# RetNet attention and a maxout FFN: last products in the order the pairs were finished, weights converted two pieces at a time

## The chip, the cores and the metric

One core of a Trainium2 chip runs the whole kernel. The metric is device time in microseconds, the median over several executions. A core has TensorE (PE; its weight loads are shown apart as PEld), VectorE (DVE), ScalarE (ACT), GpSimd (POOL), and SyncE (SP), which here only issues DMAs. Each engine executes its own list of instructions in order, and semaphores tie the lists together.

## The reference

```python
batch, n_heads, seq, head_dim = (8, 8, 576, 64)
scores = scale * np.matmul(q, k.transpose(0, 1, 3, 2))      # scale = 1/sqrt(64)
Dmat = np.where(rel >= 0, gamma[:, None, None] ** rel[None, :, :], 0.0)   # rel = i - j, one gamma per head
ret = scores * Dmat[None, :, :, :]
attn = np.matmul(ret, v)
x = attn.transpose(0, 2, 1, 3).reshape(4608, 512)
h = np.maximum(np.maximum(x @ w1, x @ w2), x @ w3)          # w1, w2, w3: (512, 768)
out = h @ w_out                                            # w_out: (768, 512)
```

q, k and v are float32. The four weight matrices are float64; the kernel gets them as 64-bit integers, the bits of the doubles, and makes float32 of them on the chip.

## The kernel before

The 4608 rows are nine tiles of 512 tokens (`t` = 0 to 8). For each tile, attention makes `xT[t]`, and `ffn(t)` makes the hidden units `h` and the output rows. The 768 hidden units are six blocks of 128, called `fb`, or three pairs of blocks, called `fp`. The order of instructions on every engine is the order in which the Python code emits them (`tc.manual_schedule()`): `ffn(t)` is a generator that emits a stretch of its own work at each step, and `steps(t + 1)` puts the attention of the next tile between the steps. TensorE goes through attention of the next tile and the FFN of this tile in turn.

**Tile 0** does plain products. For every unit (`fp`, `i`), where `i` is one of the three matrices, `up_plain` multiplies two blocks (L744), ScalarE copies the first matrix's result to `h` (L749), and VectorE takes the maximum with the next two (L748). Then `downs_plain` multiplies `h` by `w_out` (L731). Meanwhile the weights are loaded and converted, in the order in which tile 0 uses them: 24 `pieces` of 128 x 512, 18 of `w1` to `w3` and 6 of `w_out`. `load_weights` issues their DMAs from SP (L504, two for a piece; L499 for `w_out`) into six buffers named `bits`. `convert_all` is a generator that emits the conversion step by step; `convert(n)` takes n of its steps, and `ffn(0)` calls it between the blocks. One piece takes:

- VectorE, L629: `expo`, the exponent bits of the high word; ScalarE, L630: `mant` = 1 + low word x 2^-52
- ScalarE, L632 and L635: two Relus that turn `expo` into the exponent of a float32, saturating at both ends; VectorE, L634: `frac`, the top 20 fraction bits
- VectorE, L640: `mant` += `frac` x 2^-20 ("whole"); L645: the sign bit is put into `expo` ("sign"); L651: `w` = `mant` x `expo` ("product"), after which `load_weights(1)` asks for the next piece

Each is 128 x 512. The first two pieces go one by one; from the third on, two pieces get their masks first and are then finished one after the other.

**Tiles 1 to 8** use fewer products. `weight_sums`, `sums_of_x` and the list `PRODUCTS` make the three maxed products of a pair `fp` from sums of weights and of x (L720, evicted at L705, joined on VectorE at L708); the last joins of a pair end its `h`. Tile 1 does pair 1 in the plain way, and its pairs in the order 1, 0, 2; later tiles take 0, 2, 1 (`order` in `ffn`, L785). Then `sums_of_hidden` (L530 to L532) makes four sums `H1` to `H4` of h for each pair, and `downs(t, h)` makes the output with seven products of 256-wide halves (L562), in the order 1, 2, 6, 7, 5, 4, 3. Product n runs over the three pairs, in `product`; products 1, 2 and 4 read `h` itself, the others the sums:

```python
        def product(n, out, first):
            for fp in range(NF // 2):
                for m, cols, o in out:
                    nc.tensor.matmul(o, lhsT=hS[n](fp)[:, m * P:(m + 1) * P], rhs=late["T"][n][:, fp, cols], ...
```

One float32 matmul of the program appears as two passes of TensorE in the trace, so product 1 (bank `dx`) is 3 pairs x 2 blocks x 2 = 12 passes of 256 columns; in the last tile its second block is split, and there are 18.

Of the kernel before, what the change touches and what calls it, by code (L numbers as in the profile page):

```python
# [77 lines left out]
WAHEAD = 6  # L78
# [3 lines left out]
def kernel(  # L82
# [14 lines left out]
    nc = tc.nc  # L97
    P = 128
    B, H, S, D = q.shape
    N, DM = out.shape  # L100
# [4 lines left out]
    NF = DF // P  # L105
# [25 lines left out]
    one, top, inf, first = (const.tile([P, 1], FP32, name=n) for n in ("one", "top", "inf", "first"))  # L131
# [354 lines left out]
    units = [(fp, i) for fp in range(NF // 2) for i in range(3)]  # L486
    pieces = [(i, 2 * fp + e) for fp, i in units for e in range(2)] + [("out", fb) for fb in range(NF)]
    w_sb, bits, to_load = {}, {}, deque(pieces)
    w_up = [const.tile([P, NF, DM], FP32, name=f"w{i}") for i in range(3)]
    w_out = const.tile([P, NF // 2, 2, DM], FP32, name="w_out")  # L490

    def load_weights(n):
        for _ in range(n):
            if not to_load:
                return
            i, fb = piece = to_load.popleft()
            t = bits[piece] = wraw.tile([P, DM], I64, tag="bits", name="bits")
            if i == "out":
                nc.sync.dma_start(t[:], moe_w_out[fb * P:(fb + 1) * P, :])  # L499
            else:  # L500
                heads = WS[i][:, fb * P:(fb + 1) * P].rearrange("(h p) f -> p h f", p=D)
                blocks = t[:].rearrange("p (n f) -> p n f", f=P)
# [28 lines left out]
        urgent.append(lambda: vec(s2, s1, a11, op=ALU.subtract))  # L531
        urgent.append(lambda: (pool(s3, a11, a21, op=ALU.subtract), pool(s4, a12, s2, op=ALU.subtract)))  # L532

    def downs(t, h):

        def raw_hidden(r, e):
            return lambda fp: h[:, 2 * fp + e, NH * r:NH * (r + 1)]
# [19 lines left out]
            return banks.get(id(src), src)  # L557

        def product(n, out, first):
            for fp in range(NF // 2):  # L560
                for m, cols, o in out:
                    nc.tensor.matmul(o, lhsT=hS[n](fp)[:, m * P:(m + 1) * P], rhs=late["T"][n][:, fp, cols],  # L562
                                     start=first and fp == 0 and (m == 0 or last and out is x),
                                     stop=fp == NF // 2 - 1, skip_group_check=True)

        def kept(src):
            both = ppool.tile([P, NM, NH], FP32, tag="part", name="part")
# [51 lines left out]
    def convert_all():  # L619

        def masks(raw_bits):
            words = raw_bits[:].bitcast(I32).rearrange("p (f two) -> p f two", two=2)
            high = words[:, :, 1]
            low = raw_bits[:].bitcast(U32).rearrange("p (f two) -> p f two", two=2)[:, :, 0]
            expo = wtmp.tile([P, DM], I32, tag="expo", name="expo")
            mant = wtmp.tile([P, DM], FP32, tag="mant", name="mant")
            nc.vector.tensor_scalar(out=expo[:], in0=high, scalar1=0x7FF00000, scalar2=None, op0=ALU.bitwise_and)  # L629
            nc.scalar.activation(mant[:], low, AF.Identity, bias=one[:], scale=2.0 ** -52)  # L630
            yield
            nc.scalar.activation(expo[:].bitcast(FP32), expo[:], AF.Relu, bias=top[:], scale=-8.0)  # L632
            frac = wtmp.tile([P, DM], I32, tag="frac", name="frac", bufs=2)
            nc.vector.tensor_scalar(out=frac[:], in0=high, scalar1=0xFFFFF, scalar2=None, op0=ALU.bitwise_and)  # L634
            nc.scalar.activation(expo[:], expo[:].bitcast(FP32), AF.Relu, bias=inf[:], scale=-1.0)  # L635
            yield
            return high, expo, mant, frac

        def whole(mant, frac):
            nc.vector.scalar_tensor_tensor(out=mant[:], in0=frac[:], scalar=2.0 ** -20, in1=mant[:],  # L640
                                           op0=ALU.mult, op1=ALU.add)

        def product(piece, high, expo, mant):
            i, fb = piece
            nc.vector.scalar_tensor_tensor(out=expo[:], in0=high, scalar=-2 ** 31, in1=expo[:],  # L645
                                           op0=ALU.bitwise_and, op1=ALU.bitwise_or)
            if i == "out":
                w = w_sb[piece] = w_out[:, fb // 2, fb % 2, :]
            else:
                w = w_sb[piece] = w_up[i][:, fb, :]  # L650
            nc.vector.tensor_tensor(w, mant[:], expo[:].bitcast(FP32), op=ALU.mult)  # L651
            load_weights(1)

        for group in [pieces[:1], pieces[1:2]] + [pieces[n:n + 2] for n in range(2, len(pieces), 2)]:
            masked = []
            for piece in group:
                masked.append((yield from masks(bits.pop(piece))))
            for piece, (high, expo, mant, frac) in zip(group, masked):
                whole(mant, frac)
# [29 lines left out]
    def convert(n):  # L689
        for _ in range(n):  # L690
            next(converting, None)
# [59 lines left out]
    def ffn(t):  # L751

        h = hpool.tile([P, NF, NT], FP32, tag="h", name="h")
        if t == 0:
            for fp, i in units:
                for fb in (2 * fp, 2 * fp + 1):
                    maximum = up_plain(t, h, fb, i)
                    if CPT not in qks:
                        maximum()
                        transposes(CPT)  # L760
                        convert(4)
                        continue
# [204 lines left out]
```

## Time and profile before

| | |
|---|---|
| median of 4 runs | 757.37 us (756.87 to 758.52) |
| the profiled execution | 758.52 us, span 756.5 us |
| TensorE busy | 747.1 us, 99% of the span, 5928 passes |
| VectorE busy | 535.2 us, 71% |
| ScalarE busy | 342.4 us, 45% |
| GpSimd busy | 90.4 us, 12% |
| granted TensorE clock | 1.0 |
| DMA | 59.2 MB, 78 GB/s on average |

The span runs from the first to the last instruction that the profiler recorded on the core; the execution's own time is longer by 2.0 us. A row of the profile names the line of the kernel, the engine, the operation, the tile written and the tiles read, shapes, and how often; a row of the timeline begins with its start and its length in us, and may end with the engine's idle time before it and, behind the arrow, what ended that. Ends of matmuls are modelled.

### The profile page before, as it was taken

What the parts mean: (1) busy time and instruction counts of PE and PEld (TensorE: products, weight loads), DVE (VectorE), ACT (ScalarE), POOL (GpSimd) and SP (SyncE); (2) the same over time, 40 slices, a digit from 0 to 9 for tenths busy, and PEclk for the clock granted to TensorE, in tenths of its full rate; (3) what the DMA queues carried; (4) which work ended last, traced back from release to release, by engine and by line L of the source; (5) the groups of instructions that cost most, each with busy time, mean ns of one, the idle gap of its engine ahead of it and who ended that gap; (6) DMA issues with size and microseconds to landing.
All of it is one profiled execution on the core that took longest, in us unless ns stands there. A gap on an engine that the chain in (4) does not pass through costs nothing.

```text
span 756.5 us, 15101 instructions
## 1 busy us (share of the span) xinstructions
PE 747.1 (99%) x5928; PEld 608.3 (80%) x5928; DVE 535.2 (71%) x929; ACT 342.4 (45%) x700; POOL 90.4 (12%) x112
## 2 busy tenths in 40 slices
PE   8999999999999999999999999999999999999998
PEld 7645545587888888888888888888888888888887
DVE  2998997958886866686668847685768666863662
ACT  3574651255255534553355345542555255414441
POOL 3110013002010100011011102010101010100000
PEclk9999999999999999999999999999999999999999
DMA  9995752404242514242343224232514141000001
GB/s 218 222 244 127 206 126 75 94 1 80 76 88 45 91 31 105 49 73 55 72 82 66 62 62 93 49 65 66 94 31 92 43 93 35 1 30 28 1 1 55
DMA packets 230310, 59.20 MB, mean 78 GB/s; under 512 B 211168, under 2 KB 228960, under 8 KB 230240
## 3 DMA queue, kind: packets, MB, share of 16 engines
q1 hardware_dynamic: 229664, 57.91, 35.5%
q8 instruction: 46, 0.75, 0.4%
q10 hardware_dynamic: 576, 0.33, 0.2%
q14 instruction: 24, 0.20, 0.1%
HBM read 48.76 MB, written 9.44 MB: 77 GB/s over the span
## 4 chain that ended last, share of the span: by engine, by line
PE 91%; DVE 4%; ACT 1%; DMA 1%; SPq 1%; issue 1%; POOL 0%; DVEq 0%; ACTq 0%; POOLq 0%
PE a L720 16%; PE b L720 14%; PE up L744 11%; PE dx L562 11%; PE c L720 8%; PE dz L562 5%; PE e L720 5%; PE d L720 5%; PE o L438 4%; PE down L731 3%; PE dy L562 3%; PE sk L317 3%; DVE part L708 2%; SPq L218 1%; ACT part L705 1%; PE s L299 1%
## 5 line engine op out<-in xcount | busy, mean ns | idle before, releaser
L708 DVE TENSOR_TENSOR part<-part 128x512 f32<-128x512 f32 x161 | 111.2, 691 | 94.4 <-ACT part L705 92.1
L705 ACT COPY part<-b 128x512 f32<-128x512 f32 x115 | 67.4, 586 | 140.1 <-PE b L720 140.1
L708 DVE TENSOR_TENSOR h<-h,part 128x512 f32<-128x512 f32 x115 | 79.6, 692 | 28.2 <-ACT h L705 24.3
L744 PE MATMUL up<-xT,w 128*128 128x512 f32 (+2 forms) x200 | 84.7, 578 | 1.5 <-DVE w L651 1.5
L705 ACT COPY part<-a 128x512 f32<-128x512 f32 x92 | 53.9, 586 | 48.5 <-PE a L720 48.1
L744 PEld LDWEIGHTS up<-xT,w 128*128 128x128 f32 x200 | 36.8, 190 | 43.5 <-issue 38.7
L720 PE MATMUL a<-s,w 128*128 128x256 f32 x276 | 70.9, 379 | 0.0
L720 PE MATMUL b<-s,n 128*128 128x256 f32 x276 | 70.8, 379 | 0.0
L186 ACT ACTIVATE kraw<-kraw,gk 128x64 f32<-128x64 f32 x208 | 65.6, 346 | 3.6 <-DMA kraw<-in_k_dram 3.3
L720 PEld LDWEIGHTS b<-s,n 128*128 128x128 f32 x276 | 52.4, 190 | 7.1
L720 PEld LDWEIGHTS a<-s,w 128*128 128x128 f32 x276 | 52.4, 190 | 7.1
L532 POOL TENSOR_TENSOR H<-h 128x256 f32<-128x256 f32 x24 | 20.3, 844 | 285.8 <-DVE h L708 285.7
L335 POOL TENSOR_TENSOR va<-va,gs_of 64x512 f32<-64x512 f32 x24 | 25.8, 1075 | 232.2 <-DVE va L333 178.3
L720 PE MATMUL c<-xT,w 128*128 128x256 f32 x184 | 49.1, 389 | 0.0
L720 PE MATMUL d<-s,w 128*128 128x256 f32 x184 | 47.3, 380 | 0.2 <-ACT part L705 0.2
L720 PE MATMUL b<-xT,n 128*128 128x256 f32 x184 | 47.2, 379 | 0.0
L562 PE MATMUL dx<-To,H 128*128 128x256 f32 (+1 forms) x204 | 44.9, 370 | 0.0
L720 PE MATMUL e<-xT,w 128*128 128x256 f32 x184 | 43.5, 379 | 0.0
L720 PE MATMUL a<-xT,n 128*128 128x256 f32 x184 | 43.5, 379 | 0.0
L562 PEld LDWEIGHTS dx<-To,H 128*128 128x128 f32 x204 | 36.6, 190 | 4.9
L720 PEld LDWEIGHTS d<-s,w 128*128 128x128 f32 x184 | 34.9, 190 | 5.3 <-ACT part L705 0.6
L325 DVE TENSOR_TENSOR m<-sk,gm 64x512 f32<-64x512 f32 x56 | 38.5, 687 | 1.0
(122 smaller groups left out, 1338.7 us busy)
## 6 DMA issues: line engine op xcount, KB each, us to landing
bits<-in_moe_w_dram SPq DMA_DIRECT2D x36, 256.0 KB, 5.4
out_dram<-osb SPq DMA_DIRECT2D x35, 256.0 KB, 2.1
kraw<-in_k_dram SPq DMA_DIRECT2D x32, 256.0 KB, 3.0
qraw<-in_q_dram SPq DMA_DIRECT2D x224, 32.0 KB, 2.2
kxraw<-in_k_dram SPq DMA_DIRECT2D x224, 32.0 KB, 2.1
va<-in_v_dram SPq DMA_DIRECT2D x56, 128.0 KB, 3.1
bits<-in_moe_w_out_dram SPq DMA_DIRECT2D x6, 512.0 KB, 5.7
vraw<-in_v_dram SPq DMA_DIRECT2D x7, 256.0 KB, 4.8
```

Source lines behind the costliest of these rows:

```text
L186: scaling.popleft()()
L317: nc.tensor.matmul(sk[c][half(c), h, :], lhsT=kr[half(c), h, :], rhs=vas[g, c][half(c), h, :], start=True, stop=True)
L325: nc.vector.tensor_tensor(ms[g, c][half(c)], sk[1 - c][half(c)], gm[half(c)], op=ALU.mult)
L335: nc.gpsimd.tensor_tensor(to[half(1)], to[half(1)], gs_of[half(1)].unsqueeze(2).to_broadcast([D, H, D]), op=ALU.mult)
L438: nc.tensor.matmul(o[half(c), n % 2, n // 2, half(m)], lhsT=vas[g, m][:, h, :], rhs=ms[g, m][:, h, :], start=m == 0 and n == 0, stop=True, ...
L532: urgent.append(lambda: (pool(s3, a11, a21, op=ALU.subtract), pool(s4, a12, s2, op=ALU.subtract)))
L562: nc.tensor.matmul(o, lhsT=hS[n](fp)[:, m * P:(m + 1) * P], rhs=late["T"][n][:, fp, cols], start=first and fp == 0 and (m == 0 or last and ...
L705: nc.scalar.copy(of[step], ps[step[0]][:])
L708: nc.vector.tensor_tensor(of[dst], a, b, op=op)
L720: nc.tensor.matmul(ps[chain][:, e, :], lhsT=factor(w, 2 * fp + e), rhs=xS[t][x], start=n == 1 and e == 0, stop=ends, skip_group_check=True)
L731: nc.tensor.matmul(b[:], lhsT=h[:, fb, m * P:(m + 1) * P], rhs=w_sb["out", fb], start=(fb == 0), stop=(fb == NF - 1))
L744: nc.tensor.matmul(ps[:, cols], lhsT=w_sb[i, fb][:, dc * P:(dc + 1) * P], rhs=xT[t][:, dc, cols], start=dc == 0 and cols.start == 0, stop= ...
```

## The change

Two edits. In `downs`, `product` takes the pairs in the order given by `ffn`, the one in which the tile finished them, instead of 0, 1, 2; the marks for the first and the last matmul of an accumulation follow. In the conversion, the two pieces of a pair share one tile of `bits`, `expo`, `mant` and `frac`. The first four pieces are still converted with 512-wide instructions, in the same sequence as before. From the fifth piece on, every instruction covers both pieces of a pair, 1024 wide; the exponent mask of the following pair is emitted ahead of the sign and product of the present one; and `convert` is asked for fewer, larger steps. There are half as many buffers of twice the size.

```diff
-    wraw = while_converting.enter_context(tc.tile_pool(name="wraw", bufs=WAHEAD))
-    wtmp = while_converting.enter_context(tc.tile_pool(name="wtmp", bufs=4))
+    wraw = while_converting.enter_context(tc.tile_pool(name="wraw", bufs=WAHEAD // 2))
+    wtmp = while_converting.enter_context(tc.tile_pool(name="wtmp", bufs=2))
...
             i, fb = piece = to_load.popleft()
-            t = bits[piece] = wraw.tile([P, DM], I64, tag="bits", name="bits")
+            if fb % 2 == 0:
+                bits[i, fb // 2] = wraw.tile([P, 2, DM], I64, tag="bits", name="bits")
+            t = bits[i, fb // 2][:, fb % 2, :]
...
-    def downs(t, h):
+    def downs(t, h, order):
...
         def product(n, out, first):
-            for fp in range(NF // 2):
+            for fp in order:
                 for m, cols, o in out:
                     nc.tensor.matmul(o, lhsT=hS[n](fp)[:, m * P:(m + 1) * P], rhs=late["T"][n][:, fp, cols],
-                                     start=first and fp == 0 and (m == 0 or last and out is x),
-                                     stop=fp == NF // 2 - 1, skip_group_check=True)
+                                     start=first and fp == order[0] and (m == 0 or last and out is x),
+                                     stop=fp == order[-1], skip_group_check=True)
...
+        class Two:
+            def __init__(self, n):
+                self.i, fb = pieces[2 * n]
+                self.fp = fb // 2
+                words = bits.pop((self.i, self.fp))[:].rearrange("p e f -> p (e f)")
+                self.high = words.bitcast(I32).rearrange("p (e f two) -> p e f two", e=2, two=2)[:, :, :, 1]
+                self.low = words.bitcast(U32).rearrange("p (e f two) -> p e f two", e=2, two=2)[:, :, :, 0]
+                self.expo = wtmp.tile([P, 2, DM], I32, tag="expo", name="expo")
+                self.mant = wtmp.tile([P, 2, DM], FP32, tag="mant", name="mant")
+
+            def exponent(self, e):
+                expo = self.expo[:, e, :]
+                nc.vector.tensor_scalar(out=expo, in0=self.high[:, e, :], scalar1=0x7FF00000, scalar2=None,
+                                        op0=ALU.bitwise_and)
+                nc.scalar.activation(self.mant[:, e, :], self.low[:, e, :], AF.Identity, bias=one[:], scale=2.0 ** -52)
+
+            def fraction(self, e):
+                expo = self.expo[:, e, :]
+                if e != TWO[1]:
+                    self.frac = wtmp.tile([P, 2, DM], I32, tag="frac", name="frac", bufs=1)
+                nc.scalar.activation(expo.bitcast(FP32), expo, AF.Relu, bias=top[:], scale=-8.0)
+                nc.vector.tensor_scalar(out=self.frac[:, e, :], in0=self.high[:, e, :], scalar1=0xFFFFF, scalar2=None,
+                                        op0=ALU.bitwise_and)
+                nc.scalar.activation(expo, expo.bitcast(FP32), AF.Relu, bias=inf[:], scale=-1.0)
+
+            def whole(self, e):
+                nc.vector.scalar_tensor_tensor(out=self.mant[:, e, :], in0=self.frac[:, e, :], scalar=2.0 ** -20,
+                                               in1=self.mant[:, e, :], op0=ALU.mult, op1=ALU.add)
+
+            def sign(self, e):
+                nc.vector.scalar_tensor_tensor(out=self.expo[:, e, :], in0=self.high[:, e, :], scalar=-2 ** 31,
+                                               in1=self.expo[:, e, :], op0=ALU.bitwise_and, op1=ALU.bitwise_or)
+
+            def product(self, e):
+                if self.i == "out":
+                    w = w_out[:, self.fp]
+                else:
+                    w = w_up[self.i][:, 2 * self.fp:2 * self.fp + 2, :]
+                nc.vector.tensor_tensor(w[:, e, :], self.mant[:, e, :], self.expo[:, e, :].bitcast(FP32), op=ALU.mult)
+                for n in range(2)[e]:
+                    w_sb[self.i, 2 * self.fp + n] = w[:, n, :]
+                    load_weights(1)
...
+        two = Two(2)
+        two.exponent(both)
+        yield
+        two.fraction(both)
+        two.whole(both)
+        yield
+        for n in range(3, len(pieces) // 2 + 1):
+            following = Two(n) if n < len(pieces) // 2 else None
+            if following:
+                following.exponent(both)
+            two.sign(both)
+            yield
+            two.product(both)
+            yield
+            if following:
+                following.fraction(both)
                 yield
-                product(piece, high, expo, mant)
+                following.whole(both)
                 yield
+            two = following
...
-                    convert(4)
+                    convert(4 if (fp, i) == units[0] else 2)
                     maximum()
                 yield
-            convert(6)
+            convert(3)
             for fb, _ in enumerate(downs_plain(t, h)):
-                convert(4 if fb < 2 else 4 * len(pieces))
+                convert(2 if fb < 2 else 4 * len(pieces))
...
-        for n, _ in enumerate(downs(t, h)):
+        for n, _ in enumerate(downs(t, h, order)):
```

The functions that `Two` replaces are `masks`, `whole` and `product` of `convert_all`. In the prediction, "mask" is `exponent` or `fraction` on VectorE, and pair n of the conversion is the one of pieces 2n and 2n + 1, so pair 2 holds the weights of unit (0, 2), pairs 3 to 5 those of units (1, 0) to (1, 2), and pairs 9 to 11 those of `w_out`.

More of the change, by code (lines that the diff above doesn't have):

```diff
@@ L496, in load_weights @@
             i, fb = piece = to_load.popleft()
-            t = bits[piece] = wraw.tile([P, DM], I64, tag="bits", name="bits")
+            if fb % 2 == 0:
+                bits[i, fb // 2] = wraw.tile([P, 2, DM], I64, tag="bits", name="bits")
+            t = bits[i, fb // 2][:, fb % 2, :]
             if i == "out":
-                nc.sync.dma_start(t[:], moe_w_out[fb * P:(fb + 1) * P, :])
+                nc.sync.dma_start(t, moe_w_out[fb * P:(fb + 1) * P, :])
             else:
                 heads = WS[i][:, fb * P:(fb + 1) * P].rearrange("(h p) f -> p h f", p=D)
-                blocks = t[:].rearrange("p (n f) -> p n f", f=P)
+                blocks = t.rearrange("p (n f) -> p n f", f=P)
                 for c in range(2):
@@ L619, in convert_all @@
     def convert_all():
[L623 to L630, printed above, removed]
-            yield
[L632 to L635, printed above, removed]
-            yield
-            return high, expo, mant, frac
@@ L639, in whole @@
[L639 to L659, printed above, removed]
+        class Two:
[35 more added lines that the diff above has]
+                    load_weights(1)
@@ new lines, in convert_all @@
+        TWO = [slice(0, 1), slice(1, 2)]
+        both = slice(0, 2)
+        two = Two(0)
+        for e in TWO:
+            for step in (two.exponent, two.fraction, two.whole):
+                step(e)
+                yield
+            two.sign(e)
+            two.product(e)
+            yield
+        two = Two(1)
+        for e in TWO:
+            for step in (two.exponent, two.fraction):
+                step(e)
+                yield
+        for e in TWO:
+            two.whole(e)
+            yield
+            two.sign(e)
+            two.product(e)
+            yield
@@ L660, in convert_all @@
+        two = Two(2)
[3 more added lines that the diff above has]
+        two.whole(both)
+        yield
+        for n in range(3, len(pieces) // 2 + 1):
[3 more added lines that the diff above has]
+            two.sign(both)
+            yield
+            two.product(both)
+            yield
+            if following:
+                following.fraction(both)
                 yield
-                product(piece, high, expo, mant)
+                following.whole(both)
```

## The prediction

> **What bounds the kernel now.** I read the sums by stretch of time first, then the order of the engines' work in the two places that the change touches, then who waits for whom. (Columns of the first view: stretch, length, then busy time and instructions of TensorE, its weight loads, VectorE, ScalarE and GpSimd, granted clock, DMA share, GB/s.)
>
> ```profile
> 26.00:126.00 100.00, 100.00 (x485) 51.36 (x486) 92.28 (x171) 55.57 (x85) 12.87 (x15) 1.00 0.71 169
> 187.00:734.00 547.00, 546.24 (x4540) 476.91 (x4539) 376.18 (x632) 249.08 (x534) 57.53 (x67) 1.00 0.28 58
> ```
>
> From 26 us on TensorE is never idle by this account, in the first tile (26 to 126, where the weights are converted) and in the tiles from the third on alike; the clock is full. VectorE is at 92% in the first tile and still not the bound. So nothing that shortens VectorE or ScalarE is worth time by itself: the change can only win where TensorE waits inside its "busy" time, and lose where it makes TensorE wait. The ends of matmuls are modelled, so such a wait hides in the length of a row. The timeline of TensorE at the first of the last products (dx, product 1) of tiles 1, 2 and 8 (columns: start, length from first start to last end):
>
> ```profile
> 187.41 2.75 PE L562 MATMUL dx<-w_out,h 128*128 128x256 f32 x12
> ...
> 266.21 3.14 PE L562 MATMUL dx<-w_out,h 128*128 128x256 f32 x12
> ...
> 734.78 3.17 PE L562 MATMUL dx<-w_out,h 128*128 128x256 f32 x18
> ```
>
> The same twelve passes take 2.75 us in tile 1 and 3.14 us in tile 2 (3.15 in each of tiles 3 to 7). The last tile splits its bank, so it is compared with its own later dx rows of 18 passes, 2.80 us. The weight loads and VectorE of tile 2 say why:
>
> ```profile
> 266.00 0.84 PEld L562 LDWEIGHTS dx<-w_out,h 128*128 128x128 f32 x4
> 267.36 1.59 PEld L562 LDWEIGHTS dx<-w_out,h 128*128 128x128 f32 x8 [0.52 <-DVE h L708]
> ```
> ```profile
> 266.62 0.69 DVE L708 TENSOR_TENSOR h<-h,part 128x512 f32<-128x512 f32 x1
> ```
>
> Four passes (pair 0), then a wait for h, the hidden units of the pair finished last, which VectorE ends at 267.31; then the other eight. The waits in total name it once:
>
> ```profile
> PEld dx L562 <- DVE h L708: 3.5, 7, 0.5
> ```
>
> Seven tiles. Tile 1 computes pairs in the order 1, 0, 2 and takes them 0, 1, 2, so its last-finished pair already comes last, and it has no wait. Tiles 2 to 8 compute 0, 2, 1 and take 0, 1, 2.
>
> **Part one: pairs taken in the order they were finished.** In tiles 2 to 8 pair 2 comes before pair 1. That puts four more passes of 0.216 us (start to start), 0.86 us, ahead of the pair that is late. Its first weight load would be due at 267.72 (first pass 266.21, plus eight passes, less the 0.21 by which a load precedes its pass); h is there at 267.31, and in this trace the load followed it by 0.05. It is 0.36 us early: the wait goes whole, with the restart behind it. Worth 3.14 - 2.75 = 0.39 in tile 2, five times 0.40 in tiles 3 to 7, 3.17 - 2.80 = 0.37 in tile 8: 2.76 us. Next to be late is product 6, which needs H2 of pair 1: VectorE ends it at 272.09, and even 0.4 us sooner pair 1 of that product starts after 275. Product 2 uses the same h; product 7 and 4 come later still. In tile 1 the new order 1, 0, 2 keeps pair 2 last: nothing. TensorE's instructions are the same in number and shape, those of GpSimd and of the DMA queue (SP) unchanged in order.
>
> **Part two: wide conversion.** Twenty of the 24 pieces go through five VectorE and three ScalarE instructions each; now ten pairs do: 50 and 30 instructions fewer. No 1024-wide row is in the trace, so I size it from two narrow ones. VectorE tensor ops last 0.42 us at 256 and 0.69 at 512, and follow each other 0.60 apart at 512: 1024 lasts 1.22, spaced 1.13 (0.12 more when it waits for the one before). Masks last 0.42 at 512, spaced 0.33: 1024 lasts 0.68, spaced 0.60. ScalarE's 0.35 (64 wide) and 0.72 (512) give 1.15. Saved: 0.33 us of VectorE and some 0.9 of ScalarE per pair, 3.3 and 9 us in all, all of it beside TensorE's matmuls and so worth nothing.
>
> What counts is when a weight is ready. A pair's first piece now waits for the second's work, and the mask of the *next* pair stands ahead of its sign and product. The first wide pair is unit (0, 2), and it is the tight one. VectorE and TensorE there before:
>
> ```profile
> 36.82 0.42 DVE L629 TENSOR_SCALAR expo<-bits 128x512 int32<-128x512 int32 x1
> ...
> 41.02 0.69 DVE L651 TENSOR_TENSOR w<-mant,expo 128x512 f32<-128x512 f32 x1
> ...
> 43.55 0.69 DVE L651 TENSOR_TENSOR w<-mant,expo 128x512 f32<-128x512 f32 x1
> ```
> ```profile
> 43.41 7.03 PE L744 MATMUL up<-xT,w 128*128 128x512 f32 x16
> ```
>
> The first piece's weights were ready at 41.71, and TensorE began with them at 43.41. After the change, from 36.82 (nothing before it changes): mask of exponents 0.60, of fractions 0.60, whole 0.12 + 1.13, the two score masks 1.20, the state 0.33, exponents of the next pair 0.60, sign 1.13, product 0.12 + 1.22: 43.87, and a few hundredths for the added DMA waits: 43.91. ScalarE is in time (its two Relus end near 39.9, the sign is at 41.4), so are the bits (the next pair's last transfer is issued at 31.0 and takes 8.6 at most, against 40.8). TensorE's load follows by 0.05 and a restart costs 0.10, as at dx: the first pass counts from 44.05 rather than 43.41. **Cost: 0.64 us, once.**
>
> Behind the waiting TensorE everything moves 0.64 with it, so the later pairs gain that much room. Pair 3: the mask of its fractions meets GpSimd's multiply at 43.92 to 45.14, and the next exponent mask waits for bits that land near 47.5; product at 49.4, ready at 50.6; due 51.47 + 0.64 less 0.26 for load and signal, 51.85. Room 1.2. Pair 4: max, fractions, whole, max, two score masks from 50.5 to 54.75; exponents of pair 5 behind GpSimd's second multiply (54.10 to 55.19) to 55.74; sign, product: ready at 58.2, due 58.8. Room 0.6. Pair 5 is due at 69; from there VectorE has waited for TensorE (2.74 us at 69.16), and the walk leaves 2.5 at pair 6 and 1 to 2 at pair 9.
>
> Evictions: the max for unit (0, 1) slips from 41.63 to 43.82, ScalarE's copy of the first unit from 38.65 to about 40; their PSUM banks are wanted at 51.5 and 46.8: 7 and 6 us of cover. Loads: both pieces of a pair now wait for both old pieces to be read, which moves the first from 29.02 to 29.07; the next two wait behind a v transfer till 39.2 anyway, and the pair after for a sign that ends at 42.65 where the queue arrives at 42.95. No transfer is later.
>
> [...] First, a mask at 512 that normally takes 0.42:
>
> ```profile
> 44.15 1.27 DVE L629 TENSOR_SCALAR expo<-bits 128x512 int32<-128x512 int32 x1
> ```
>
> It met GpSimd's multiply. [...] I put 0.39 us for it into pair 4; without it the room there would be 1.0, with it 0.6. Neither is a wait, so the sum stays at 0.64. [...] By full durations the walk ends at 36.82 + 0.68 + 0.68 + 1.22 + 2 x 0.69 + 0.42 + 0.68 + 1.22 + 1.22 = 44.32, the wait is 1.06 and the net -1.7; by the rows -2.1. I take the rows, as they are this stretch's own; 1.06 stays the upper end. Were the fixed part of a wide row wholly hidden, the walk ends 0.3 sooner: 0.3 is the lower end.
>
> **Sum.** -2.76 + 0.64 = -2.1 us. The profiled execution took 758.52 with a span of 756.5: span 754.4, its own time 756.4. It was the slowest of the four shown, 1.15 above their median of 757.37; on the median I expect 755.3.
>
> **The rivals.** (a) *More than one new wait.* Room of 0.6 at pair 4 and 1.2 at pair 3 rests on wide rows that nobody has timed here; transfers 1 us later, or masks blocked once more, make pair 4 late by some 1 us on top: net -1.1, 756.3 (755.9 to 757). For it: VectorE is at 92%; against: each wait moves TensorE and makes room for the next. Chance 0.20. (b) *Slower: wide VectorE instructions dearer than two narrow ones*, by x each, in the first tile. Sixteen of them stand between 36.82 and the product of pair 4; 1.1 us of that is absorbed where masks would wait for GpSimd or bits anyway. TensorE's wait there becomes 16x - 1.1 us. It eats the gain of 2.76 at x = 0.24; at 0.5 (a mask losing its fast rate costs 0.53) it is 6.9, net +4.1, 761.5. Against: 256 to 512 wide costs no more than proportionally, and the 1.27 above is a collision, not a price. Chance 0.08. (c) *The order brings nothing*, because h, or what follows product 1, holds TensorE anyway: +0.64, 758.0. Against: tile 1 shows the same products without the wait, and the margin is 0.36. Chance 0.06.
>
> **How the numbers follow.** About 0.2% (1.5 us) is what a measurement can tell here. My forecast, chance 0.66: 754.9 to 755.9 by the ends of the wait (0.3 to 1.1), and half a us of measurement around it; nine tenths of it is faster by over 0.2%. Rival (a) is mostly within 0.2%, (c) within, (b) slower, and some of (b)'s chance and a stray hundredth or two make 0.10. Faster 0.62, same 0.28, slower 0.10. The range 754.4 to 757.5 holds the forecast and (a) and leaves out (b) and (c).
>
> **What would show it.** Right: the dx row of tiles 2 to 7 at 2.75 us, weight loads of dx no longer waiting for h; one wait of TensorE for the product of the first wide pair, 0.4 to 1 us, near 43.4; wide rows of about 1.22 and 0.68 us. Wrong: waits at the units that start near 51.5, 58.4 or 99.7; dx rows still over 3 us; a wide row well over twice the narrow one.

## The result, and the profile after

The changed kernel takes 756.57 us (median of 34 runs, 754.60 to 757.77) against 757.66 us of the kernel before in the same comparison (56 runs, 756.73 to 760.27): a ratio of 0.9981, 95% interval 0.9976 to 0.9987. That is 1.4 us (1.0 to 1.8) less. (The ratio is that of the means; the medians lie 1.1 us apart.) The prediction had said 755.3 us, 2.1 us less, and a range of 754.4 to 757.5. The profiled execution took 756.41 us, against 758.52 before.

From the page of the profile after (span, then busy time, share and instructions of three engines):

```profile
span 754.7 us, 15014 instructions
...
PE 746.2 (99%) x5928; PEld 608.4 (81%) x5928; DVE 529.7 (70%) x879; ACT 336.6 (45%) x670; POOL 91.0 (12%) x112
```

VectorE has 50 instructions and 5.5 us less, ScalarE 30 and 5.8 us less, and TensorE is as full as before. (The prediction had put these savings at 3.3 and 9 us: both are off, and neither counts, for none of this is time by itself.) What changed is where TensorE waits inside its rows.

**The gain.** The timeline of TensorE, and that of its weight loads, at the first of the last products in tiles 2 and 8:

```profile
266.83 2.75 PE L564 MATMUL dx<-w_out,h 128*128 128x256 f32 x12
...
733.34 2.80 PE L564 MATMUL dx<-w_out,h 128*128 128x256 f32 x18
```
```profile
266.62 2.56 PEld L564 LDWEIGHTS dx<-w_out,h 128*128 128x128 f32 x12
```

All twelve weight loads stand in one unbroken row, without the wait for h in their midst, and the row of passes has the length of tile 1's. The rows of tiles 2 to 7 are 2.75 us each, that of tile 8 is 2.80.

**The cost.** The timeline of TensorE in the first tile, at the unit (0, 2) whose weights are the first wide pair. (The transposes qt come just ahead of it. The first fence is the kernel before, where the unit began 0.43 us after the start of that row, at 43.41; the second is the changed kernel.)

```profile
42.98 0.60 PE L285 MATMUL qt<-ident,qraw 128*128 128x128 f32 x4
```
```profile
41.90 0.63 PE L285 MATMUL qt<-ident,qraw 128*128 128x128 f32 x4 [0.26 <-DMA qraw<-in_q_dram]
43.47 1.98 PE L790 MATMUL up<-xT,w 128*128 128x512 f32 x4 [0.94 <-DVE w L663]
```

Now it begins 1.57 us after it, for the product of the pair. Start to start is the safe measure here, because the rows overlap (in the kernel before, qt ends at 43.58 and the unit begins at 43.41): 1.57 - 0.43 = 1.14 us of wait. VectorE on the way to that product, and later at pair 4:

```profile
36.13 0.68 DVE L646 TENSOR_SCALAR frac<-bits 128x1024 int32<-128x1024 int32 x1
37.35 1.23 DVE L651 SCALAR_TENSOR_TENSOR mant<-frac,mant 128x1024 f32<-128x1024 int32 x1 [0.53 <-DVE frac L646]
...
40.33 0.70 DVE L637 TENSOR_SCALAR expo<-bits 128x1024 int32<-128x1024 int32 x1 [0.22 <-DMA bits<-in_moe_w_dram]
...
42.19 1.22 DVE L663 TENSOR_TENSOR w<-mant,expo 128x1024 f32<-128x1024 f32 x1
...
54.91 1.53 DVE L637 TENSOR_SCALAR expo<-bits 128x1024 int32<-128x1024 int32 x1
```

Two things on the way were not in the prediction's walk: a stop of 0.53 us between the mask of fractions and the sum (the walk had 0.12), though both of the sum's inputs are there, and 0.22 us for bits. The row at 54.91 is the mask of pair 5 in front of pair 4's product, 0.69 us long when it is alone; GpSimd's multiply runs beside it:

```profile
54.85 1.04 POOL L253 TENSOR_TENSOR vd<-vraw,gk 128x512 f32<-128x512 f32 x1 [10.53 <-DMA vraw<-in_v_dram]
```

The two overlap for 0.98 us (54.91 to 55.89), and the mask takes 0.84 us longer. The product of pair 4 ends at 58.83, and TensorE waits 0.3 us for it at unit (1, 1), and 0.10 for the restart. The sizes of the wide rows are as predicted (groups of the profile: count, then busy us and mean ns):

```profile
L663 DVE TENSOR_TENSOR w<-mant,expo 128x1024 f32<-128x1024 f32 x7 | 8.6, 1225 | 0.2
L645 ACT ACTIVATE expo<-expo,top 128x1024 f32<-128x1024 int32 x10 | 11.4, 1144 | 12.7 <-DVE expo L637 12.7
```

One caution for comparing the two profiles directly. TensorE began the first unit at 24.34 us instead of 25.89, because a transfer of q landed earlier in that execution (a variation: other builds with the same code up to there began between 24.3 and 27.8). That head start is lost again by 43.47, where TensorE stands level with before (43.41), since the waits in between end at a landing of q and at VectorE's product. The runs, not this pair of traces, have to say what each part is worth.

### The profile page after: what moved, and what is told of

The parts are those of the page before. It is cut to its first block, busy times and chain, and to the rows that moved or that the text cites. A ratio compares the mean times of both kernels' runs of the same rounds, so it can differ in the third digit from the quotient of the medians.

```text
span 754.7 us, 15014 instructions
## 1 busy us (share of the span) xinstructions
PE 746.2 (99%) x5928; PEld 608.4 (81%) x5928; DVE 529.7 (70%) x879; ACT 336.6 (45%) x670; POOL 91.0 (12%) x112
## 4 chain that ended last, share of the span: by engine, by line
PE 91%; DVE 3%; SPq 2%; DMA 2%; ACT 1%; issue 1%; POOL 0%; DVEq 0%; POOLq 0%; ACTq 0%
PE a L766 18%; PE b L766 15%; PE dx L564 11%; PE c L766 8%; PE up L790 7%; PE dz L564 5%; PE d L766 5%; PE e L766 5%; PE o L438 4%; PE down L777 3%; PE dy L564 3%; PE sk L317 3%; DMA bits<-in_moe_w_dram 1%; SPq L218 1%; SPq L247 1%; PE sk L321 1%
```

## The experiments

Theory: the order gives its 2.76 us in full, and the conversion costs about 1.3 us, because the product of a wide pair comes too late for TensorE at pair 2 and at times at pair 4. Rivals: the order gives less and the conversion costs nothing; or the cost lies in the width, not in what stands ahead of the product.

All ratios are to the kernel before on the same chip, with their 95% intervals. "qt to up" is the start-to-start time at unit (0, 2), 0.43 where nothing waits; "mask to sum" the idle time of VectorE between the mask of fractions and the sum of the first wide pair.

| kernel | ratio | qt to up, us | mask to sum, us |
|---|---|---|---|
| changed kernel | 0.9981 (0.9976 to 0.9987) | 1.57 | 0.53 |
| order alone | 0.9961 (0.9948 to 0.9974) | 0.43 | none wide |
| wide conversion alone | 1.0021 (1.0008 to 1.0034) | 1.46 | 0.53 |
| pairs reversed | 1.0101 (1.0085 to 1.0116) | 0.44 | none wide |
| mask behind the product | 0.9970 (0.9959 to 0.9981) | 0.87 | 0.53 |
| mask behind, product in halves | 0.9972 (0.9962 to 0.9983) | 0.43 | 0.52 |
| wide from the seventh piece | 0.9979 (0.9968 to 0.9989) | 0.43 | 0.11 |
| masks of the first wide pair in halves | 0.9981 (0.9972 to 0.9989) | 1.17 | 0.11 |
| memset of inf twice | 0.9991 (0.9979 to 1.0003) | 1.05 | 0.10 |
| memset of top twice | 0.9979 (0.9970 to 0.9987) | 0.79 | 0.12 |
| a tile of 16 bytes more | 1.0089 (1.0076 to 1.0102) | - | 0.52 |

### The order alone

```diff
-            for fp in range(NF // 2):
+            for fp in order:
```

(with its marks for first and last, in the kernel before)

> The order part alone: the kernel before, with product taking the pairs in the order in which the tile finished them; the conversion as before. Theory (the order gives its full 2.76 us, and the wide conversion costs about 1.3 us in the first tile): 2.76 us below the kernel before, a ratio of 0.9964, so faster than the changed kernel (0.9981); dx rows of tiles 2 to 7 at 2.75 us. Rival (the order gives only what the changed kernel shows net, because the rest comes back as a wait in later tiles, and the conversion costs nothing): 1.4 us below, 0.9981.

755.30 us (median of 8) against 758.17: 3.0 us less (2.0 to 3.9). TensorE's row in tile 2, in the timeline of this kernel:

```profile
265.86 2.75 PE L562 MATMUL dx<-w_out,h 128*128 128x256 f32 x12
```

The theory holds, the rival falls. This version beats both kernels; its interval and that of the changed kernel do not overlap, though only just (0.9974 and 0.9976).

### The wide conversion alone

```diff
-        for n, _ in enumerate(downs(t, h, order)):
+        for n, _ in enumerate(downs(t, h, range(NF // 2))):
```

> The conversion part alone: the changed kernel with product taking the pairs 0, 1, 2 again. Theory: TensorE waits for the products of pairs 2 and 4 of the first tile by some 1.3 us in all, and nothing gives it back: a ratio of 1.0017. The prediction's own size (one wait of 0.64 us): 1.0008. Rival (the conversion costs nothing): 1.0000. The dx rows of tiles 2 to 7 stay at 3.14 us.

759.96 us against 758.17: 1.6 us more (0.6 to 2.6). The prediction's own 0.64 is at the edge of the interval, zero is outside it. TensorE at unit (0, 2) in its timeline:

```profile
42.14 0.60 PE L285 MATMUL qt<-ident,qraw 128*128 128x128 f32 x4
43.60 7.13 PE L790 MATMUL up<-xT,w 128*128 128x512 f32 x16 [0.87 <-DVE w L663]
```

No bits and no q are late here, and the wait is 1.46 - 0.43 = 1.03 us. It is the only one: unit (1, 1), where the theory had expected a second, begins without a wait. From the transposes ahead of unit (0, 2) (row kt) to the first row behind the last products of tile 0, TensorE takes 82.47 us in this trace and 81.34 in each of the three narrow kernels (before, order alone, reversed): 1.13 us, the wait and its restart. That is within the interval of the runs, which also has room for further waits. In the changed kernel's trace the same stretch takes 83.42 us, of which 0.46 is a late q: waits at pairs 2 and 4, 1.6 us.

The two parts add up: -3.0 + 1.6 = -1.4, what the changed kernel gives.

### The pairs reversed

```diff
-        for n, _ in enumerate(downs(t, h)):
+        for n, _ in enumerate(downs(t, h, order[::-1])):
```

(the order part alone, with the pair finished last taken first)

> Dose of the order: the kernel before, with product taking the pair that was finished last first. Theory: a pair's place in the row is worth its four passes, 0.86 us; the first weight load of dx is due at 266.00 in the trace of before and h is there at 267.31, so TensorE waits 0.86 us more than before in tiles 2 to 8, and newly by about 1 us in tile 1, whose last pair came last before: some 7 us above, 1.009; dx rows of tiles 2 to 7 near 4.0 us, or a longer gap ahead of them. Rival (time that TensorE gains or loses at dx is taken back by waits behind it): under 3 us above, below 1.004.

766.15 us against 758.17: 7.7 us more (6.4 to 8.8). TensorE in tile 2, and its wait in total, from the list of waits:

```profile
268.36 2.83 PE L562 MATMUL dx<-w_out,h 128*128 128x256 f32 x12 [1.08 <-DVE h L708]
```
```profile
PE dx L562 <- DVE h L708: 8.6, 8, 1.1
```

Eight waits, tile 1 included. From one dx row to the next it is now 80.12 us (tiles 2 to 3), against 79.19 before: 0.93 us a tile for moving the late pair from the middle to the front, about the 0.86 us of the four passes that no longer stand ahead of it. Nothing behind the products takes any of it back.

### The mask behind the product

```diff
-            if following:
-                following.exponent(both)
             two.sign(both)
             yield
             two.product(both)
+            if following:
+                following.exponent(both)
             yield
```

> The changed kernel with the exponent mask of the following pair emitted behind the product of the present one instead of ahead of its sign and product. Theory (the new waits come from that mask, which waits for the bits of the next pair and for GpSimd's multiply while the product stands behind it): the product of pair 2 comes 0.6 to 0.8 us sooner, pair 4's some 1.5 us sooner, of the 1.3 us some 0.9 go, and the ratio falls from the changed kernel's 0.9981 to about 0.9969. Rival (the width itself makes the wait: the first piece waits for the second's work): the product of pair 2 still comes after TensorE wants it, and the ratio stays at 0.998. A third way: the masks, now late, delay ScalarE and the next pair's product, and pairs 3 and 4 wait instead: 0.998 or above.

0.9970, as the theory said (0.9959 to 0.9981; the interval still meets that of the changed kernel). In its timeline the wait at unit (0, 2) falls from 1.03 to 0.87 - 0.43 = 0.44 us:

```profile
42.93 0.60 PE L285 MATMUL qt<-ident,qraw 128*128 128x128 f32 x4
43.80 7.13 PE L790 MATMUL up<-xT,w 128*128 128x512 f32 x16 [0.27 <-DVE w L663]
```

That is the 0.60 us of one mask. So over half of the wait came from the mask's place. The stop of 0.53 us is still there, and so is finishing both pieces at once; the 0.44 us that is left goes when the product is halved (next experiment), and the stop alone is worth 0.42 (7.58 against 7.16 us, below). Unit (1, 1) begins without a wait here.

### The product in halves

```diff
-            two.product(both)
+            for e in (TWO if n == 3 else [both]):
+                two.product(e)
             if following:
                 following.exponent(both)
```

(on top of the kernel just above)

> The variant with the mask of the following pair behind the product (0.9970), and in addition the product of the first wide pair taken in two halves of 512, so that TensorE may start with the first piece. Theory (what is left there, 0.44 us, is the wait for the end of that wide product): the half ends 0.55 us sooner than the whole, the wait is 0 to 0.05 us, and the ratio falls to about 0.9965, the order's own gain. Rival (TensorE then waits for something else, the second half or pair 3): 0.9970.

The wait at unit (0, 2) is gone:

```profile
44.92 0.60 PE L285 MATMUL qt<-ident,qraw 128*128 128x128 f32 x4
45.35 7.03 PE L791 MATMUL up<-xT,w 128*128 128x512 f32 x16
```

And yet the ratio is 0.9972, no better than 0.9970. In this trace the time comes back at pair 4, as the rival had it. VectorE there:

```profile
57.31 2.06 DVE L655 SCALAR_TENSOR_TENSOR expo<-bits,expo 128x1024 int32<-128x1024 int32 x1
59.41 1.23 DVE L663 TENSOR_TENSOR w<-mant,expo 128x1024 f32<-128x1024 f32 x1
```

The sign, 1.22 us when it is alone, meets GpSimd's multiply (57.25 to 58.29) and takes 2.06; TensorE waits 0.31 us at unit (1, 1) and 0.10 at the restart. In the kernel just above the same clash (2.10 us) costs TensorE nothing: there it had waited 0.44 us at pair 2, and VectorE came to the sign 0.35 us sooner after the unit's transposes (12.04 us, here 12.39). The two intervals cannot tell the kernels apart; that the time comes back is the trace's account.

### Wide only from the seventh piece

```diff
-        two = Two(1)
-        for e in TWO:
...
+        for n in (1, 2):
+            two = Two(n)
+            for e in TWO:
...
-        two = Two(2)
+        two = Two(3)
...
-                    convert(4 if (fp, i) == units[0] else 2)
+                    convert(4 if (fp, i) in units[:2] else 2)
```

> The changed kernel, 1024 wide only from the seventh piece on: the pair for unit (0, 2) is converted as in the kernel before, with masks of both pieces and then one piece after the other. Theory (all but some 0.3 us of the conversion's cost is the wait for the product of the first wide pair): TensorE does not wait at unit (0, 2), at most 0.3 us at unit (1, 1); ratio 0.9964 to 0.9968, as with the order alone (0.9961). Rival (the next pair that is wide becomes the late one, since VectorE is behind by then): about 1 us of wait at unit (1, 0), ratio 0.9978 or above.

No wait at unit (0, 2), 0.26 us at unit (1, 1) as expected, and a further 0.26 at 102 us, at the products of w_out, that was not. By the trace that is 2.76 - 0.52 = 2.2 us less, 0.9970; the runs say 0.9979, with 0.9970 inside the interval, above what was expected. Some 14 us earlier VectorE had waited 2.5 us for bits of w_out (list of waits):

```profile
DVE expo L637 <- DMA bits<-in_moe_w_out_dram: 2.5, 1, 2.5
```

This wait is in the trace of every wide kernel (1.2 to 3.6 us), and in none of the narrow ones (before, order alone, reversed). It does not take a later transfer: the bits of the first w_out pair had landed at 87.41 us in the kernel before and at 86.72 in the changed one. But the narrow kernel reads them with masks at 90.12 and 94.33 us, and the changed kernel's VectorE comes to its one mask for both at 85.01. The mask of a wide pair needs the transfers of both its pieces and stands in front of the product of the pair before; so it waits for bits while weights whose own bits have long been there wait behind it. In the changed kernel's trace these 1.80 us cost TensorE nothing.

### What is the stop of 0.53 us

It stood at the same spot, with 0.52 or 0.53 us, in all five kernels with the same list of VectorE up to there, however their transfers landed. It matters for the wait at pair 2: without it the first wide product comes 0.4 us sooner. The first test splits the two masks of that pair, which moves the sum two places on:

```diff
-        two.exponent(both)
+        for e in TWO:
+            two.exponent(e)
         yield
-        two.fraction(both)
+        for e in TWO:
+            two.fraction(e)
         two.whole(both)
```

> The changed kernel with the masks of the first wide pair (unit (0, 2)) taken in two halves of 512, for exponents and for fractions; two instructions more on VectorE and two on ScalarE, everything else 1024 wide as before. It is about the 0.53 us in which VectorE stands between the mask of fractions and the sum of that pair in the changed kernel and in both of its variants so far, though mant and frac are there; no later pair shows it (0.10). Theory A (it belongs to a place in VectorE's list of instructions, and anything queued there hides it): the sum follows the last mask by about 0.1 us, the product of the pair comes some 0.3 us sooner, after 0.12 for the narrower masks; ratio about 0.9977, against 0.9981 of the changed kernel. Theory B (it belongs to the first wide sum itself): the 0.53 us stay in front of it, and the ratio is 0.9982 or 0.9983.

VectorE in its timeline:

```profile
37.41 0.76 DVE L646 TENSOR_SCALAR frac<-bits 128x512 int32<-128x512 int32 x2
38.28 1.23 DVE L651 SCALAR_TENSOR_TENSOR mant<-frac,mant 128x1024 f32<-128x1024 int32 x1
```

The stop is gone, as theory A said; the ratio, 0.9981 (0.9972 to 0.9989), cannot tell 0.9977 from 0.9982. The kernel that is wide from the seventh piece has its first wide sum elsewhere in the list, and no stop either:

```profile
45.55 0.69 DVE L646 TENSOR_SCALAR frac<-bits 128x1024 int32<-128x1024 int32 x1
46.35 1.22 DVE L651 SCALAR_TENSOR_TENSOR mant<-frac,mant 128x1024 f32<-128x1024 int32 x1
```

Two kernels with one idle instruction and with three, run once each:

```diff
     nc.vector.memset(one[:], 1.0)
+    idle = const.tile([P, 4], FP32, name="idle")
+    for n in range(1):          # 3 in the second
+        nc.vector.memset(idle[:, n:n + 1], 0.0)
```

> The changed kernel with one idle instruction more on VectorE at its very start (a memset of one column that nobody reads), to see what the 0.53 us in front of the first wide sum belong to. Theory A (a place in VectorE's list of instructions): everything behind moves on by one place, the stop now falls between the mask of fractions and the wait that stands in front of the sum, or on that wait, and 0.5 us stay in front of the sum. Theory B (that sum itself): 0.53 as well. One look at the trace; a single time says nothing at this size.

> The same with three idle memsets. Theory A: the stop falls on a mask, which is handed to VectorE while the one before it still runs (0.60 us each), so that it is hidden wholly or but for some 0.1 to 0.2 us; the sum follows the mask of fractions by 0.10, and TensorE's wait at the first wide pair is 0.4 us shorter than with the stop. Theory B: 0.53 us stay in front of the sum.

The stop is gone in both (0.10 to 0.11 us). For one instruction I had expected 0.5: wrong, and why is not shown. But these kernels took 765.89 and 763.80 us against 759.30 in single runs, with late transfers (in the lists of waits ScalarE stands 20.1 and 20.7 us for bits of `w1` to `w3`, 10.8 in the changed kernel), and so could say nothing on time. Was that the instruction, or the new tile? The two were then parted:

```diff
     nc.vector.memset(inf[:], 255.0 * 2.0 ** 23)
+    nc.vector.memset(inf[:], 255.0 * 2.0 ** 23)
```

> The changed kernel with one idle instruction more at the start of VectorE's list, but without a new tile: the memset of inf is made twice. (The two kernels before had a new tile of 16 bytes a partition for it, and took 4 to 7 us more; this one leaves every address as it is.) Theory A (the 0.53 us belong to a place in VectorE's list): the stop falls one place earlier, on the wait between mask and sum, while the mask still runs for 0.69 us; the sum follows the mask by 0.10, TensorE's wait at the first wide pair is about 0.4 us shorter than with the stop, ratio about 0.9975. Theory B (that sum itself): 0.53 as before and 0.9981. If the new tile cost nothing and the time came from the added instruction: 1.004 or more.

```diff
     nc.vector.memset(one[:], 1.0)
+    const.tile([P, 4], FP32, name="idle")
```

> The changed kernel with that new tile of 16 bytes a partition alone, which nothing reads or writes: every tile made after it stands 16 bytes or more further on. If the 4 to 7 us came from the addresses: a ratio of 1.003 to 1.008, with DMA landings later and TensorE waiting in the first tile; the 0.53 us stay in front of the first wide sum, since VectorE's list is the same. If they came from the added instructions or from those single runs: 0.998.

```diff
     nc.vector.memset(top[:], 1151.0 * 2.0 ** 23)
+    nc.vector.memset(top[:], 1151.0 * 2.0 ** 23)
```

> As the kernel before it, with the memset of top made twice instead of that of inf: again one place more in VectorE's list and no address moved. It is there because that kernel lost the stop as expected and yet gave 0.9991: its trace shows the bits of the first w_out pair landing 1.9 us later than in the changed kernel, and TensorE waiting 1.3 us for the last weights behind them. If that lateness is a chance of its executions: the ratio here is 0.9970 to 0.9980, no wait of TensorE near 100 to 103 us, and 0.10 between mask and sum. If the moved place itself makes these transfers late: 0.999 again, with the same waits. If the stop belongs to the first wide sum: 0.53 us in front of it.

With a memset twice, VectorE and TensorE (inf twice):

```profile
37.14 0.69 DVE L647 TENSOR_SCALAR frac<-bits 128x1024 int32<-128x1024 int32 x1
37.93 1.23 DVE L652 SCALAR_TENSOR_TENSOR mant<-frac,mant 128x1024 f32<-128x1024 int32 x1
```
```profile
42.69 0.60 PE L285 MATMUL qt<-ident,qraw 128*128 128x128 f32 x4
43.74 7.13 PE L791 MATMUL up<-xT,w 128*128 128x512 f32 x16 [0.45 <-DVE w L664]
```

No stop, and a wait at unit (0, 2) of 1.05 - 0.43 = 0.62 us. From the first mask of the pair to the end of its product it is now 7.16 us in both (36.53 to 43.69, 36.71 to 43.87), where the kernel with the wide conversion alone takes 7.58. So the stop belongs to a place in VectorE's list: an instruction whose result nobody reads, 36 us earlier, takes it away.

The traces show which place. Count the rows that they keep of VectorE, waits on semaphores included: in all five kernels with the stop, the sum behind it is row 64. The same search in all fourteen traces, for 0.4 us or more of idle time after everything that the instruction waited for had ended, finds (apart from 1.65 us at the kernel's last output) rows 64, 448 and 832 in four of these five, row 64 in the split product, row 1088 in the three narrow kernels, and none in the other six. Every one is a multiple of 64. This is the one at row 448 of the changed kernel:

```profile
271.04 0.69 DVE L754 TENSOR_TENSOR h<-h,part 128x512 f32<-128x512 f32 x1 [0.46 <-DVE h L754]
```

Other multiples of 64 show no such idle time. What happens at these rows is not shown.

No time was won for it. With inf twice the ratio is 0.9991 (0.9979 to 1.0003) where 0.9975 was expected; with top twice it is 0.9979, at the edge of what was expected (0.9970 to 0.9980) and not apart from the changed kernel's 0.9981. With inf twice, TensorE waited 1.33 us between 99.7 and 104 us, behind a mask that waited 3.56 us for bits of w_out; with top twice 0.60 at pair 4, behind bits 1.44 us late, and 0.77 ahead of 104.5, where none was expected if the late bits were chance. Whether these landings are late by chance, or because VectorE's list has moved, the two runs do not say.

The tile alone, 6.9 us slower than the kernel before (1.0089, a little over the 1.008 expected) and with the stop in place, is the subject of the last section.

## Why the prediction was right, and where it was off

**The order: right in mechanism, place and size.** 2.76 us were summed from the dx rows, 3.0 (2.0 to 3.9) measured with the order alone. The rows have the length that tile 1 had shown, product 6 did not become late, and the reversed order shows that the late pair's place costs about what four passes cost (0.93 us a tile, 0.86 by the passes). Rival (c), that something else holds TensorE there, is out.

**The wide rows: right.** 1.22 us for sums and products, 0.69 for masks, 1.15 on ScalarE. Rival (b), dearer wide instructions, is out. Nothing that was saved on VectorE and ScalarE came back as time, as stated: the wide conversion alone is slower than the kernel before.

**The mis-sized term: "Cost: 0.64 us, once".** The mechanism is as told: TensorE waits at unit (0, 2) for a product behind the next pair's mask. The size failed in two steps.

The first is "mask of fractions 0.60, whole 0.12 + 1.13". The trace has 0.53 us of idle time where the walk had 0.12. Without that stop the wait measures 0.62 us and its restart 0.10, near the walk's 0.64; with it, 1.03 and 0.10. No row in that stretch of the trace before showed it, and neither of the two ways of adding up the walk would have given it (by full durations the wait was to be 1.06; that this is near the measured number is luck, for the rows follow each other as predicted, 0.60 and 1.13 to 1.14 us apart). No run shows the ground of the lower end of 0.3 either, wide rows closer together than that.

The second is "once", which rested on "Room 0.6" at pair 4. In the changed kernel TensorE waits there too, 0.3 us and the restart: one of the prediction's own signs of being wrong. Two terms took the room. The clash with GpSimd cost 0.84 us instead of 0.39. And TensorE began unit (1, 0) at 51.62 us instead of 52.11 (51.47 + 0.64), with its head start, while VectorE was held till 47.58 by bits that landed at 47.46, as foreseen ("near 47.5"). Both differ from trace to trace: in that of the wide conversion alone the mask loses 0.17 us, and pair 4 does not wait. "No transfer is later" held within 0.6 us in that pair of traces. What the walk left out is that a mask that comes sooner waits for the same transfer: 0.22 us ahead of pair 2's product, where the last bits landed 0.56 us later than before, and 1.80 at the first w_out pair, where they landed 0.7 us sooner.

So the conversion costs 1.6 us (0.6 to 2.6) by the runs. 1.1 of it is the wait at pair 2 in the trace of the conversion alone, 0.5 more than predicted; the rest differs from trace to trace, at pair 4 or at the products of w_out, and how often it comes in the runs is not shown. "Each wait makes room for the next" is half true: the split product takes the wait at pair 2 away and pair 4 waits, but the changed kernel waited 1.14 us at pair 2 and 0.4 at pair 4 all the same.

Rival (a) is the nearer account: more than one wait, with a mask lengthened once more (1.53 us against 0.69), though not with transfers 1 us later. Its 756.3 is nearer to the 756.57 measured than the 755.3 of the forecast, and the forecast's own -2.1 us lies outside the interval of the result (1.0 to 1.8 less). The range held it because it had been drawn to take in (a).

**The clash with GpSimd.** The prediction gave it 0.39 us of pair 4's room and no wait. That was an estimate beside one row, the mask of 1.27 us instead of 0.42, which lost 0.85 of the 0.99 us that it shared with the multiply. The later traces have 0.84 for a mask (1.53 against 0.69) and for a sign (2.06 against 1.22), each beside a multiply of 1.04 with which it overlaps for 0.98: most of the overlap is lost, though not all. The share was right, since 0.39 had been given for an overlap of 0.44; the meeting of the two was misplaced. The walk had the multiply start 0.65 us ahead of the mask, and it started 0.06 ahead.

## What to carry to other kernels

Take first what was finished first: where a sum over blocks may run in any order, the order of production cost nothing here and removed the wait at the seam (dx rows of 2.75 us instead of 3.14). Widening instructions on an engine that is not the bound won nothing here and gathered waits: the wider step needs all of its inputs (1.80 us of waiting for bits at the first w_out pair of the changed kernel), and what stood ahead of the first result that the bound engine wanted, above all the mask of the next pair, became that engine's wait (1.03 us at unit (0, 2), 0.44 with the mask behind the product). Test the parts of a change apart: here one part gave 3.0 us and the other took 1.6 back.

## What the runs showed of the hardware

**A tile of 16 bytes a partition, which nothing touches, made the changed kernel some 8 us slower** (1.0089 of the kernel before, 1.0076 to 1.0102, where the changed kernel has 0.9981): by the edit, every tile made after it stands further on in memory; the traces show no addresses. The DMA queue of the whole execution, changed kernel and that one (packets, MB, share of the engines' time), and the loads of bits (count, KB, median us from issue to landing):

```profile
q1 hardware_dynamic: 229664, 57.91, 35.4%
...
bits<-in_moe_w_dram SPq DMA_DIRECT2D x36, 256.0 KB, 5.0
```
```profile
q1 hardware_dynamic: 229664, 57.91, 38.0%
...
bits<-in_moe_w_dram SPq DMA_DIRECT2D x36, 256.0 KB, 6.8
```

The same packets and bytes take longer. It is lost in the first tile, where the DMA engines are busiest (a mean share of 0.95 till 26 us and 0.99 from there till 60 in the changed kernel, 1.06 and 1.09 in this one): TensorE leaves that tile at 133.47 us instead of 124.43, all of the 8.7 us by which the spans differ. The granted clock is 0.93 in the first 26 us, 1.00 in the changed kernel. That the addresses do it is concluded from the edit, which changes nothing else; what it is about them was not tried. A control kernel for this one must therefore leave every address in place, or it measures these 8 us as well.

**VectorE stood for half a us at fixed places of its list**, here always at a multiple of 64 rows (64, 448, 832, 1088; 0.43 to 0.52 us after its inputs were there). In the changed kernel each of its three such rows waits on a semaphore; one to three instructions more in the list took the stop away (0.10 to 0.12 us in its place). The profile has transfers of instructions, 16 or 8 KB each; in the changed kernel one begins 0.45, 0.66 and 1.06 us behind the end of its three stops (at 37.80, 271.70 and 532.29 us). But the kernel before has one at 39.28 us with no stop in sight, and whether the two belong together is not shown.
